# A chunked state-space scan followed by a GELU layer: a rewritten order of steps, and one small product moved to another PSUM bank

## The chip, the cores and the metric

One Trainium2 chip, one of its cores. The metric is the device time of one execution in microseconds (us), lower is better. The engines are TensorE (PE in the profile, with its weight loads apart as PEld), VectorE (DVE), ScalarE (ACT), GpSimd (POOL) and SyncE (SP), which here issues nearly all transfers. Each engine takes its own instructions strictly in the order in which the program was written; the engines wait for one another by semaphores.

## What is computed

A state-space scan over 4 batches, 8 heads and 768 positions, in chunks, with its state carried from chunk to chunk, and then a two-layer network with a GELU on the result. Cut to what matters (the reference's chunk is 32; the kernel uses 128, which gives the same sums):

```python
cum = np.cumsum(log_a[:, :, sl], axis=-1)
L = np.exp(cum[:, :, :, None] - cum[:, :, None, :]) * causal
M = np.einsum('bhin,bhjn->bhij', Cc, Bc) * L
y_intra = np.einsum('bhij,bhjd->bhid', M, xc)
y_inter = np.einsum('bhin,bhnd->bhid', Cc, state) * np.exp(cum)[:, :, :, None]
y[:, :, sl] = y_intra + y_inter
state = decay_full[:, :, None, None] * state + np.sum(Bx, axis=2)
...
h = x @ w_in                # x: y as [3072, 256]; w_in [256, 2048]
g = 0.5 * h * (1.0 + np.tanh(c * (h + 0.044715 * h * h * h)))
out = g @ w_out             # w_out [2048, 256]
```

## The kernel before

Positions are taken in 24 chunks of 128, two chunks to a *unit* u of 256 tokens (12 units, three to a batch). The decays are folded into B and C: C is scaled by the reciprocal of the running product of `a` and B by the product itself, so that the scan of a chunk becomes plain matrix products with a triangular mask.

The kernel schedules itself by hand. Each piece of work is a named *step*. The text `ORDERED` (L19) lists some 600 of them, and the loop at L924 issues them in that order; a suffix `:A`, `:D`, `:P`, `:S` picks ACT, DVE, POOL or SP for a step that can run on several. `~n` issues filler matmuls on TensorE, n units of 128 columns of zeros into the bank `yb` (`fill`, L693); `s1.0.2+4` puts four such units into that step's own bank first. The order within an engine is thus the order of the list, and a step that stands behind a waiting one on its engine waits too. A semaphore wait covers the real dependences, and the bank that a step writes must have been read by those who used it before.

The PSUM banks around the change: two `hp` banks, used in turn by the decay product, the first x and D blocks and all groups of stage 1; one `o_ps` bank (outputs); `ga` and `gb` (G and transposes); one bank `yb` (fillers and Y).

The steps that the text speaks of, with unit u, chunk c = 2u+k and group i:

- `XX.u` (L563) unpacks x of a unit of the first batch by matmul, `XD.u` (L573) adds its state update next to it in the same banks; `xn.c` copies x out to bf16 (L578). A matmul into a bank waits for the reads that were issued before it.
- `G.u` (L595) is C times B, `M.u.0`, `M.u.1` (L605, DVE) apply the triangular mask to its two halves; for unit 0 the second half goes over ACT (`GE`) and POOL (`ME`).
- `S` (L674, L676, DVE) updates the state of a chunk, `SP` (L683, DVE) prepares it for the next chunk.
- `Y.u` (L650 the part from the state, L659 the part within the chunk) writes `yb`; `yev.u` evacuates it to `xm`, the input of stage 1.
- `s1.u.i` (L709) is one of eight groups of four matmuls of the first layer into an `hp` bank, `gelu.u.i` (L713, ACT) empties it; `s2.u.k.q` (L727) is one of four groups of four matmuls of the second layer for a chunk; `oev` copies a finished output, `store` writes it.
- `wi.q.k`, `wo.q.k` cast a part of w_in and w_out to bf16 once it has landed; `castx.u` does so for x.
- `R` (L331) is the long scan of decays, `pe` (L385, L387) the products that start from it, `pp` (L393) spreads them over the partitions on TensorE, `pend` copies them out of PSUM. They are first needed for chunk 4.
- `tp2`, `tp6` (L342), `recip1` (L374), `mul1` (L435), `T1` (L443), `bh1`, `ce1`, `N1`, `bn1` turn decays, scale and transpose B and C of chunks 4 and 5 of the first batch; `mul`, `T`, `E`, `N`, `bn`, `F` do so for batches 2 to 4, where the last two go through DRAM (`store_s`, `turn_s`, `load_s`).

Of these, `s1.u.*` needs `yev.u`, `Y.1` needs `M.1.0`, `M.1.1`, `xn.2`, `xn.3`, `SP.1` and `SP.2`, and `T1.0` needs `mul1.0`, which needs `tp2`.

Of the kernel before, what the change touches and what calls it, by code (L numbers as in the profile page):

```python
# [24 lines left out]
load_bc1.0 xn.2:A ME.3:P ME.2:P pe Y.0 XD.1 pp yev.0.0.2:A S.1.0 load_wo.1 load_bc1.1 SP.1 S.1.1  # L25
load_wo.2 wi.1.1:P M.1.0 wi.2.0:P wo.0.0:D pend:A wo.0.1:P wi.2.1:P SP.2 wi.1.0:A M.1.1 s1.0.0
gelu.0.0 s1.0.1 gelu.0.1 xn.3:A wi.3.1:P s1.0.2+4 gelu.0.2 s1.0.3 s2.0.0.0.o load_wo.3 wo.1.0:P
gelu.0.3 load_bc.1.0 s1.0.4 wi.3.0:A s1.0.5 gelu.0.4 Y.1 tp2 mul1.0 gelu.0.5 yev.1.0.2:A s1.0.6
s1.0.7 gelu.0.6 load_x.2 tp6.0 load_bc.1.1 load_x.3 gelu.0.7 recip1 T1.0 s2.0.1.0.o s1.1.0 bh1:D N1
s1.1.1 wo.1.1:A tp6.3 s2.0.0.1.o wo.2.1:P gelu.1.0 gelu.1.1 mul1.1 tp6.2 T1.1 tp6.1 ce1.1:A ce1.0:A  # L30
wo.2.0:A bn1:D recip.1.4 s2.0.1.1.o s1.1.2 s1.1.3 gelu.1.2 wo.3.0:A wo.3.1:P G.2 gelu.1.3 s2.0.0.2.o
s2.0.1.2.o s2.0.0.3.o castx.2.None:P s2.0.1.3.o load_bc.2.1 M.2.0 mul.1.0 M.2.1 oev.1:A s1.1.4
s1.1.5 T.1.0 load_x.4 oev.0:A s2.1.0.0.o castx.3.None:P s2.1.0.1.o gelu.1.4 SP.3 D.2 gelu.1.5 s1.1.6
S.2.0 SP.4 load_x.5 E.1.0:A N.1 mul.1.1 bn.1:D gelu.1.6 s1.1.7 Y.2 s2.1.0.2.o T.1.1 gelu.1.7
yev.2.0.2:A s1.2.0 s1.2.1 gelu.2.0 E.1.1:D F.1 s2.1.0.3.o s1.2.2 gelu.2.1 gelu.2.2 D.3 load_bc.2.0
oev.2:D G.3 S.3.0 S.3.1 s2.1.1.0.o load_x.6 castx.4.None:P s1.2.3 gelu.2.3 s2.1.1.1.o s2.1.1.2.o
s1.2.4 M.3.1 M.3.0 gelu.2.4 SP.6 s2.1.1.3.o s1.2.5 oev.3:A gelu.2.5 D.4 Y.3 mul.2.1 S.4.0 G.4 s1.2.6
s2.2.0.0.o SP.7 castx.5.None:A yev.3.0.2:A gelu.2.6 S.4.1 s1.2.7 mul.2.0 s2.2.0.1.o s1.3.0
s2.2.0.2.o gelu.2.7 M.4.0 M.4.1 load_x.8 store_s.2.1 gelu.3.0 s1.3.1 s2.2.0.3.o s1.3.2 G.5 gelu.3.1
SP.8 gelu.3.2 store_s.2.0 D.5 Y.4 M.5.1 oev.4:A S.5.0 s1.3.3 s2.2.1.0.o s2.2.1.1.o gelu.3.3 s1.3.4  # L40
s1.3.5 s2.2.1.2.o yev.4.0.2:D s2.2.1.3.o SP.9 SP.10 gelu.3.4 gelu.3.5 s1.3.6 oev.5:A turn_s.2.1
s1.3.7 gelu.3.6 store.1 s2.3.0.0.o M.5.0 gelu.3.7 s2.3.0.1.o store.4 load_s.2 turn_s.2.0 load_x.7
store.0 store.3 store.2 castx.6.None:A s2.3.0.2.o s2.3.0.3.o s1.4.0 gelu.4.0 oev.6:A D.6
castx.7.None:P F.2 Y.5 G.6 S.6.0 S.6.1 s1.4.1 SP.13 s1.4.2 gelu.4.1 s2.3.1.0.o s2.3.1.1.o gelu.4.2
s1.4.3 s1.4.4 M.6.0 M.6.1 gelu.4.3 s2.3.1.2.o s2.3.1.3.o gelu.4.4 oev.7:A s1.4.5 s1.4.6 gelu.4.5
gelu.4.6 yev.5.0.2:D SP.12 s2.4.0.0.o s2.4.0.1.o s1.4.7 D.7 Y.6 G.7 gelu.4.7 load_bc.3.0 load_bc.3.1
mul.3.0 mul.3.1 S.7.0 S.7.1 load_x.9 s1.5.0 gelu.5.0 s2.4.0.2.o s2.4.0.3.o oev.8:A M.7.1
castx.8.None:A M.7.0 s1.5.1 s1.5.2 gelu.5.1 store_s.3.1 yev.6.0.2:D SP.14 s2.4.1.0.o s2.4.1.1.o
s1.5.3 gelu.5.2 s2.4.1.2.o s1.5.4 s2.4.1.3.o gelu.5.3 gelu.5.4 oev.9:A s1.5.5 D.8 Y.7 gelu.5.5
store_s.3.0 load_x.10 load_x.11 store.5 G.8 S.8.0 s1.5.6 s1.5.7 castx.9.None:D gelu.5.6 M.8.1  # L50
gelu.5.7 store.6 s2.5.0.0.o s2.5.0.1.o turn_s.3.0 s1.6.0 s1.6.1 s2.5.0.2.o s2.5.0.3.o gelu.6.0
gelu.6.1 oev.10:D SP.16 s1.6.2 s1.6.3 gelu.6.3 gelu.6.2 s2.5.1.0.o s2.5.1.1.o s2.5.1.2.o s2.5.1.3.o
load_s.3 store.9 turn_s.3.1 s1.6.4 s1.6.5 M.8.0 yev.7.0.2:A oev.11:A SP.15 store.8 gelu.6.4
s2.6.0.0.o F.3 s2.6.0.1.o gelu.6.5 s1.6.6 s1.6.7 gelu.6.6 Y.8 D.9 G.9 S.9.0 SP.18 S.9.1 store.7
gelu.6.7 s2.6.0.2.o s2.6.0.3.o castx.11.None:D oev.12:D s1.7.0 s1.7.1 s2.6.1.0.o gelu.7.0 s2.6.1.1.o
gelu.7.1 s1.7.2 s1.7.3 s2.6.1.2.o s2.6.1.3.o SP.19 oev.13:D M.9.0 gelu.7.2 M.9.1 castx.10.None:P
gelu.7.3 s1.7.4 s1.7.5 s2.7.0.0.o s2.7.0.1.o gelu.7.4 s1.7.6 gelu.7.5 yev.8.0.2:A s2.7.0.2.o s1.7.7
gelu.7.6 Y.9 D.10 S.10.0 S.10.1 G.10 gelu.7.7 M.10.0 s2.7.0.3.o yev.9.0.2:A oev.14:A s1.8.0 s1.8.1
s2.7.1.0.o s2.7.1.1.o gelu.8.0 gelu.8.1 SP.20 s1.8.2 s1.8.3 M.10.1 gelu.8.2 s2.7.1.2.o s2.7.1.3.o
gelu.8.3 s1.8.4 s1.8.5 Y.10 oev.15:A gelu.8.4 D.11 S.11.0 G.11 gelu.8.5 s1.8.6 store.15 s1.8.7  # L60
gelu.8.6 s2.8.0.0.o s2.8.0.1.o gelu.8.7 store.11 store.10 s1.9.0 gelu.9.0 s1.9.1 s2.8.0.2.o
s2.8.0.3.o gelu.9.1 M.11.1 M.11.0 oev.16:D SP.21 SP.22 yev.10.0.2:A s1.9.2 s1.9.3 gelu.9.2
s2.8.1.0.o s2.8.1.1.o gelu.9.3 s1.9.4 store.14 s1.9.5 gelu.9.4 s2.8.1.2.o s2.8.1.3.o gelu.9.5 s1.9.6
# [24 lines left out]
def kernel(  # L88
# [219 lines left out]
    DT, MT, RP = {}, {}, {}  # L308
# [80 lines left out]
            in1=m8.rearrange("p (j o) -> p j o", o=1).to_broadcast([64, 2 * batch, HC]), op=ALU.mult)  # L389

    def f_pp():
        RP[2] = psh.tile([128, 512], FP32, name="hp")
        nc.tensor.matmul(out=RP[2][:, 0:NCH], lhsT=selp[0:64].rearrange("p h n -> p (h n)"),  # L393
                         rhs=pe2.rearrange("p j c -> p (j c)"), start=True, stop=True,
                         skip_group_check=True)
# [567 lines left out]
```

## Time and profile before

| | |
|---|---|
| time, median of 3 runs | 117.17 us (117.15 to 117.68) |
| profiled execution, first to last instruction | 115.1 us; the page gives no other time of it |
| TensorE busy | 109.4 us, 95% |
| ACT, DVE, POOL busy | 75.1, 68.7, 15.1 us |
| chain that ended last, by engine | PE 82%, DMA 8%, SP queue 4% |
| granted TensorE clock, mean | 1.000 |
| TensorE busy in 10.00 to 14.18 us | 3.36 of 4.18 us |
| last output copied out of PSUM from | 112.11 us |

The span runs from the first to the last instruction; the time of a run is longer by what lies around it, 2.1 us if the execution was a median one. A row of the timeline gives start, length, engine, line, operation, written and read tiles, shapes and count; a bracket says how long the engine had been idle before, and who released it. Rows of TensorE overlap, since a matmul's end is that of its last result, while the next is already under way; the pace is read from the starts.

### The profile page before, as it was taken

The numbers are of one execution on the slowest core, as the hardware profiler recorded it, in microseconds if no ns is written. First come the engines' busy times: TensorE is split into PE (matmuls) and PEld (weight loads), VectorE is DVE, ScalarE is ACT, GpSimd is POOL, SyncE is SP. The second block draws the span as 40 slices with busy tenths as digits, with TensorE's granted clock in tenths as the row PEclk, the third lists the DMA queues.
The fourth block names the chain that finished last, engine by engine and source line by source line (L and its number), as shares of the span: only waits on it lengthen the run. The fifth ranks groups of instructions, "written<-read, shape, count | busy, mean of one in ns | idle before, by whom it ended". The sixth has DMA issues, their size and how long they took to land.

```text
span 115.1 us, 3372 instructions
## 1 busy us (share of the span) xinstructions
PE 109.4 (95%) x1425; PEld 92.2 (80%) x1425; DVE 68.7 (60%) x135; ACT 75.1 (65%) x149; POOL 15.1 (13%) x32
## 2 busy tenths in 40 slices
...
GB/s 65 236 280 286 397 293 311 278 84 218 225 109 226 214 64 203 192 147 265 102 158 184 174 178 0 6 0 0 0 50 138 0 49 139 0 0 51 46 103 79
DMA packets 43006, 15.97 MB, mean 139 GB/s; under 512 B 36656, under 2 KB 41456, under 8 KB 42992
## 3 DMA queue, kind: packets, MB, share of 16 engines
q1 hardware_dynamic: 42848, 15.68, 53.9%
q8 instruction: 11, 0.18, 0.6%
q10 hardware_dynamic: 144, 0.08, 0.4%
q14 instruction: 3, 0.02, 0.1%
...
## 4 chain that ended last, share of the span: by engine, by line
PE 82%; DMA 8%; SPq 4%; POOL 1%; issue 1%; ACT 0%
PE hp L709 36%; PE o_ps L727 33%; DMA wf<-in_moe_w_out_dram 8%; PE yb L727 3%; PE ga L595 3%; PE yb L650 2%; PE yb L659 2%; SPq L190 1%; PE hp L628 1%; SPq L162 1%; SPq L159 1%; SPq L150 1%; POOL w_out_sb L316 1%; POOL w_in_sb L316 1%; SPq L183 1%
## 5 line engine op out<-in xcount | busy, mean ns | idle before, releaser
L713 ACT ACTIVATE gT<-hp 128x512 bf16<-128x512 f32 x96 | 53.3, 595 | 24.5 <-PE hp L709 24.0
L709 PE MATMUL hp<-xm,w_in_sb 128*128 128x256 bf16 x384 | 51.9, 273 | 0.5 <-ACT pend L314 0.3
L727 PE MATMUL o_ps<-w_out_sb,gT 128*128 128x256 bf16 x352 | 46.4, 273 | 0.0
L709 PEld LDWEIGHTS <-w_in_sb 128*128 128x128 bf16 x384 | 41.2, 114 | 3.2 <-issue 1.7
L727 PEld LDWEIGHTS <-gT 128*128 128x128 bf16 x384 | 37.0, 98 | 4.7 <-issue 0.8
L318 DVE COPY o_sb<-o_ps 128x256 f32<-128x256 f32 x7 | 3.0, 424 | 22.4 <-PE o_ps L727 18.4
L605 DVE TENSOR_TENSOR m<-ga,tri 128x1024 bf16<-128x1024 f32 x12 | 14.6, 1216 | 0.0
L605 DVE TENSOR_TENSOR m<-gb,tri 128x1024 bf16<-128x1024 f32 x11 | 13.4, 1219 | 0.5 <-PE gb L595 0.5
L697 PE MATMUL yb<-wz 128*128 128x512 bf16 (+2 forms) x24 | 8.2, 491 | 1.1 <-DVE warm L222 1.1
L314 ACT ACTIVATE o_sb<-o_ps 128x256 f32<-128x256 f32 x15 | 5.6, 382 | 4.1 <-PE o_ps L727 3.0
L683 DVE SCALAR_TENSOR_TENSOR sp_new<-s_new,pend,bmask 128x256 bf16<-128x256 f32 x17 | 8.0, 479 | 0.1
L316 POOL CAST x<-x_t 128x512 bf16<-128x512 f32 x5 | 3.2, 648 | 34.9 <-DMA x_t<-in_x_dram 22.9
L676 DVE SCALAR_TENSOR_TENSOR s_new<-s_new,pend,hp 128x64 f32<-128x64 f32 x13 | 3.6, 279 | 5.7 <-PE hp L628 5.5
L697 PEld LDWEIGHTS <-wz 128*128 128x128 bf16 x25 | 2.9, 126 | 5.0 <-issue 3.6
L659 PE MATMUL yb<-m,x 128*32 128x128 bf16 x192 | 6.1, 219 | 0.0
L650 PE MATMUL yb<-ce,sp_new 128*32 128x128 bf16 x160 | 5.3, 220 | 0.0
L595 PE MATMUL ga<-ce,bh 32*128 32x256 bf16 x48 | 4.7, 272 | 0.1
L314 ACT ACTIVATE xm<-yb 128x512 bf16<-128x512 f32 x8 | 4.8, 597 | 0.0
L595 PE MATMUL gb<-ce,bh 32*128 32x256 bf16 x48 | 4.7, 273 | 0.0
L727 PE MATMUL yb<-w_out_sb,gT 128*128 128x256 bf16 x32 | 4.1, 273 | 0.0
L659 PEld LDWEIGHTS <-x 128*32 128x32 bf16 x192 | 3.8, 97 | 0.4 <-issue 0.2
L650 PEld LDWEIGHTS <-sp_new 128*32 128x32 bf16 x160 | 3.0, 96 | 1.0 <-issue 1.0
...
## 6 DMA issues: line engine op xcount, KB each, us to landing
...
wf<-in_moe_w_in_dram SPq DMA_DIRECT2D x4, 512.0 KB, 8.3
wf<-in_moe_w_out_dram SPq DMA_DIRECT2D x4, 512.0 KB, 8.9
...
x_t<-in_x_dram SPq DMA_DIRECT2D x1, 512.0 KB, 4.8
```

The source lines that it names most:

```text
L314: nc.scalar.activation(o, i, AF.Copy)
L316: nc.gpsimd.tensor_copy(out=o, in_=i)
L595: nc.tensor.matmul(out=gbank(g)[:, 256 * k:256 * k + 256], lhsT=bh_of(2 * u + k)[gs], rhs=ce_of(2 * u + k)[gs], start=True, stop=True, til ...
L605: nc.vector.tensor_tensor(out=m_of(u)[:, 2 * i:2 * i + 2].rearrange("p g k e t -> p (g k e) t"), in0=gx[i].rearrange("p g (k t) -> p (g k) ...
L650: nc.tensor.matmul(out=y4[32 * j:32 * j + 32, k, w], lhsT=sp[:, 32 * h:32 * h + 32], rhs=ce_of(gc)[:, h % 2], start=first(j), stop=False, ...
L659: nc.tensor.matmul(out=y4[32 * j:32 * j + 32, k, w], lhsT=X16[u][:, k, 32 * h:32 * h + 32], rhs=m[:, h // 2, h % 2, :], start=first(j), st ...
L676: nc.vector.scalar_tensor_tensor(out=s_new, in0=state[("s", gc - 1)], scalar=pend_of(gc), in1=d, op0=ALU.mult, op1=ALU.add)
L683: nc.vector.scalar_tensor_tensor(out=sp_new.rearrange("p (g d) -> p g d", g=4), in0=(XN[0][:, H * D:H * D + 64] if gc == 0 else state[("s" ...
L697: nc.tensor.matmul(out=t[:, 0:m * 128], lhsT=wz, rhs=w3.to_broadcast([128, m, 128]), start=True, stop=True, skip_group_check=True)
L709: nc.tensor.matmul(out=hp[:, j * T:(j + 1) * T], lhsT=w_in_k[:, w, q, k], rhs=xm[:, w, u * T:(u + 1) * T], start=(w == 0), stop=(w == 1))
L713: nc.scalar.activation(gts[u][:, 2 * i:2 * i + 2], hps.pop((u, i)).rearrange("p (j t) -> p j t", j=2), AF.Gelu_apprx_tanh)
L727: nc.tensor.matmul(out=ops[gc], lhsT=gts[u][:, fi, k * Q:(k + 1) * Q], rhs=w_out_sb[:, fi, :], start=(fi == 0 and (u > 0 or k == 0)), stop ...
```

## The change

Two things. The product `pp` writes the bank `yb` instead of taking an `hp` bank:

```diff
     def f_pp():
-        RP[2] = psh.tile([128, 512], FP32, name="hp")
+        RP[2] = yb
...
-    pp.takes("hp", pd)
+    pp.takes("yb", pd)
```

And the table `ORDERED` is another from the step `xn.0` on, its fifth line, to the end. Some copies and casts also change their engine in it. Its first changed line, before and after:

```diff
-XD.0 load_wo.0 xn.0:A ew.1.2:A SP.0 S.0.0 xn.1:A wi.0.0:A wi.0.1:A R ~13 G.1 S.0.1 load_wi.3 XX.1
+XD.0 load_wo.0 xn.0:A ~6 ~4 ew.1.2:A ~7 SP.0 ~4 ME.3:P S.0.0 xn.1:A ME.2:P S.0.1 wi.0.1:A Y.0
```

What that does to the engines shows in their instructions. First TensorE, between `XD.0` and the first `Y` (`wz` are the zeros of the fillers, `bh` and `ce` the scaled B and C of `G.1`); the difference, - before and + after:

```order
 L697 MATMUL yb<-wz 128x512
 L697 LDWEIGHTS wz
+L697 MATMUL yb<-wz 128x256
+L697 LDWEIGHTS wz
 L697 MATMUL yb<-wz 128x512
 L697 LDWEIGHTS wz
 L697 MATMUL yb<-wz 128x512
 L697 LDWEIGHTS wz
-L697 MATMUL yb<-wz 128x128
-L595 LDWEIGHTS bh_137
-L595 MATMUL ga<-ce_135,bh_137 128x256
```

The fillers there grow from 13 to 21 units, and `G.1`, which stood behind them, is gone from this place. TensorE's steps were `G.1 XX.1 Y.0 XD.1 pp s1.0.0 s1.0.1 s1.0.2+4 s1.0.3 s2.0.0.0 s1.0.4 s1.0.5 Y.1 s1.0.6 s1.0.7 T1.0` and are now `Y.0 XX.1 XD.1 G.1 s1.0.0 pp s1.0.1 s1.0.2+4 s1.0.3 s1.0.4 s1.0.5 Y.1 s1.0.6 s1.0.7 s2.0.0.0 T1.0`.

Next DVE from the first state update to the masks of unit 1 (`s_new` is S, `sp_new` SP, `r_t` R, `pe` the decay products, `x_407` written by xn.2, `m` the mask's result, `rt` a part of tp6):

```order
 L674 COPY s_new<-o_ps 128x64
+L676 SCALAR_TENSOR_TENSOR s_new<-s_new,pendq,hp 128x64
+L683 SCALAR_TENSOR_TENSOR sp_new<-s_new,pendq,bmask 128x256
 L331 SCALAR_TENSOR_TENSOR r_t<-ac,ends 64x384
-L676 SCALAR_TENSOR_TENSOR s_new<-s_new,pendq,hp 128x64
 L385 TENSOR_TENSOR pe_111<-ac,r_t 64x3
 L387 TENSOR_TENSOR pe_112<-pe_111,m_117 64x24
 L676 SCALAR_TENSOR_TENSOR s_new<-s_new,pendq,hp 128x64
+L318 CAST x_407<-hp 128x256
 L683 SCALAR_TENSOR_TENSOR sp_new<-s_new,pendq,bmask 128x256
+L605 TENSOR_TENSOR m<-ga,tri 128x1024
+L605 TENSOR_TENSOR m<-gb,tri 128x1024
```

`S.0.1` and `SP.1` moved ahead of the scan `R`, the copy `xn.2` came over from ACT, and the two masks of unit 1 now follow one another; a cast of w_out that stood between them went to POOL, and one of w_in (`wi.3.1`) came from POOL, behind `S.1.1` and ahead of `tp2`.

Last ACT from the second x copy on (`x_305`, `x_343` and `x_407` are x in bf16 of units 0, 1 and, in the new program, 1; `xm` is written by yev, `gT` by the GELUs):

```order
 L314 ACTIVATE x_305<-hp 128x256
-L314 ACTIVATE w_in_sb<-wf 128x512 x2
-L314 ACTIVATE x_343<-hp 128x256
+L314 ACTIVATE w_in_sb<-wf 128x512
 L314 ACTIVATE xm<-yb 128x2x2x128
-L314 ACTIVATE pend<-hp 128x2x4x3
 L314 ACTIVATE w_in_sb<-wf 128x512
-L713 ACTIVATE gT<-hp 128x512 x2
-L314 ACTIVATE x_343<-o_ps 128x256
-L713 ACTIVATE gT<-hp 128x512 x2
-L314 ACTIVATE w_in_sb<-wf 128x512
+L713 ACTIVATE gT<-hp 128x512
```

One cast of w_in and the copy `xn.2` no longer stand ahead of `yev.0`, and `pend` went behind the fourth GELU. POOL now casts four parts of w_in first (`wi.0.0`, `wi.1.1`, `wi.2.1`, `wi.2.0`), then `wo.0.0`, `wi.3.0` and five of w_out. SP's list is the same in both.

94 lines of the change are left out of this document (47 added, 47 removed).

## Prediction

> **What bounds the kernel now.** I read the table of engine busy time by stretches first, because one number for the whole span hides where TensorE (PE) stands still. The columns are the stretch, its length, then busy microseconds and instruction counts of PE, PEld, DVE, ACT and POOL, and at the end the granted clock, DMA share and GB/s.
>
> ```profile
> 14.18:18.95 4.77, 4.27 (x61) 3.38 (x60) 4.70 (x10) 4.32 (x9) 2.95 (x5) 1.00 1.01 282
> 18.95:112.00 93.05, 93.05 (x1212) 82.89 (x1204) 53.53 (x91) 63.29 (x123) 4.92 (x8) 1.00 0.49 116
> ```
>
> From 18.95 us to the last matmul PE never idles: 93.05 of 93.05 us. A new order can win nothing there, it can only lose. All that can be won lies before 18.95, so the second view is the timeline of PE, and after it the chain of work that ended last for the pace of one stage-1 pair.
>
> ```profile
> 13.25 0.18 PE L573 MATMUL hp<-x4b,bc0s 32*32 32x64 bf16 x1 [0.46 <-ACT x L314]
> ...
> 14.18 1.03 PE L709 MATMUL hp<-xm,w_in_sb 128*128 128x256 bf16 x8 [0.28 <-ACT pend L314]
> ...
> 15.46 0.38 PE L697 MATMUL hp<-wz 128*128 128x512 bf16 x1 [0.25 <-ACT gT L713]
> ...
> 17.51 0.96 PE L709 MATMUL hp<-xm,w_in_sb 128*128 128x256 bf16 x7 [0.25 <-POOL w_in_sb L316]
> ...
> 18.39 0.29 PE L650 MATMUL yb<-ce,sp_new 128*32 128x128 bf16 x8
> ...
> 18.95 1.06 PE L709 MATMUL hp<-xm,w_in_sb 128*128 128x256 bf16 x8
> ...
> 19.85 0.28 PE L443 MATMUL ga<-ident,bc0s 128*128 128x128 bf16 x2
> ```
>
> ```profile
> 22.54 0.87 PE hp L709 x8
> ```
>
> The brackets are the stalls: XD.1 waits 0.46 for xn.2 (13.25), s1.0.0 waits 0.28 (14.18), the filler in s1.0.2 waits for a GELU (15.46), s1.0.4 waits for the cast wi.2.1 on POOL (17.51). The last row says that eight stage-1 matmuls, two groups, take 0.87: a group is 0.44, and a group of stage 2 has the same shape.
>
> My ruler is **the start of T1.0, 19.85**. Before it, both orders have issued exactly the same useful PE work (s1.0.0 to s1.0.7, pp, Y.1, s2.0.0.0), and after it exactly the same is left. So the end moves by as much as T1.0 moves, plus any new stall behind it. The sum is made on this execution, span 115.1; the median of the runs is 117.17, 2.1 more lies around the span, and I move both by the same amount.
>
> **The change, part by part: PE up to s1.0.0.** Spacings of the same blocks in the trace:
>
> ```profile
> 9.08 0.28 PE L595 MATMUL ga<-ce,bh 32*128 32x256 bf16 x2
> ...
> 9.41 0.28 PE L697 MATMUL yb<-wz 128*128 128x256 bf16 x1
> ...
> 9.63 0.28 PE L563 MATMUL o_ps<-x4b,unp 32*128 32x256 bf16 x1
> ...
> 10.16 0.20 PE L573 MATMUL o_ps<-x4b,bc0s 32*32 32x64 bf16 x1
> ...
> 10.40 0.88 PE L697 MATMUL yb<-wz 128*128 128x512 bf16 x4
> ...
> 13.49 0.40 PE L393 MATMUL hp<-pe,selp 64*128 64x24 f32 x2
> ```
>
> and the ACT rows that hand over to PE:
>
> ```profile
> 11.19 0.39 ACT L314 ACTIVATE x<-hp 128x256 bf16<-128x256 f32 x1
> ...
> 11.78 1.15 ACT L314 ACTIVATE w_in_sb<-wf 128x512 bf16<-128x512 f32 x2 [0.19 <-DMA wf<-in_moe_w_in_dram]
> ...
> 14.81 1.09 ACT L713 ACTIVATE gT<-hp 128x512 bf16<-128x512 f32 x2 [0.17 <-PE hp L709]
> ```
>
> Until 10.40 nothing moves, and SP issues all transfers in one order in both kernels, so that I keep the landings of the trace. The fillers there grow from 13 to 21 units of 128 columns; a unit is 0.87/16 = 0.054, so they end at 10.40 + 1.14 = 11.54. Eight units more cost 0.44 of PE, hidden, because Y.0 waits for xn.1 anyway, which ends at 11.58. PE follows ACT by 0.05 (first GELU of the 14.81 pair ends near 15.41, filler at 15.46): Y.0 starts at 11.63. It has three sets of eight where Y.1 has four in 0.56 (18.39 to 18.95): 0.42. Then XX.1 at 12.05, XD.1 0.53 later (9.63 to 10.16) at 12.58, G.1 0.24 later at 12.82, s1.0.0 0.33 later (9.08 to 9.41) at **13.15 instead of 14.18**. XD.1 no longer waits for xn.2, since that copy now stands behind it. Its input is ready: ACT has one cast less ahead of yev.0, so yev.0 runs from about 12.4 to 13.0; wi.0.0 moved to POOL, which is free then. That is 1.03 gained so far.
>
> **The change, part by part: what DVE gives back.** DVE now does S.0.1, SP.1, R, pe, S.1.0, xn.2, SP.2, M.1.0, M.1.1, tp6.0, S.1.1, wi.3.1, tp2, recip1, mul1.0 in this order. Its rows before, and the group row for a copy like xn.2:
>
> ```profile
> L318 DVE COPY o_sb<-o_ps 128x256 f32<-128x256 f32 x7 | 3.0, 424 | 22.4 <-PE o_ps L727 18.4 <-ACT gT L713 4.0
> ```
>
> ```profile
> 11.47 0.21 DVE L674 COPY s_new<-o_ps 128x64 f32<-128x64 f32 x1
> 11.60 0.94 DVE L331 TENSOR_TENSOR_SCAN r_t<-ac,ends 64x384 f32<-64x384 f32 x1
> 12.46 0.25 DVE L676 SCALAR_TENSOR_TENSOR s_new<-s_new,pendq,hp 128x64 f32<-128x64 f32 x1
> 12.63 0.15 DVE L385 TENSOR_TENSOR pe<-ac,r_t 64x3 f32<-64x3 f32 x1
> 12.82 0.18 DVE L387 TENSOR_TENSOR pe<-pe,m 64x24 f32<-64x24 f32 x1
> 13.80 0.28 DVE L676 SCALAR_TENSOR_TENSOR s_new<-s_new,pendq,hp 128x64 f32<-128x64 f32 x1 [0.81 <-PE o_ps L573]
> 14.00 0.48 DVE L683 SCALAR_TENSOR_TENSOR sp_new<-s_new,pendq,bmask 128x256 bf16<-128x256 f32 x1
> ...
> 14.59 1.22 DVE L605 TENSOR_TENSOR m<-ga,tri 128x1024 bf16<-128x1024 f32 x1
> ...
> 15.80 0.43 DVE L318 CAST w_out_sb<-wf 128x512 bf16<-128x512 f32 x1
> ...
> 18.14 0.99 DVE L342 STREAM_TRANSPOSE rt<-r_t 32x64 f32<-32x64 f32 x4
> 19.16 0.52 DVE L435 TENSOR_TENSOR bc0s<-bcf,rt 128x256 bf16<-128x256 f32 x1
> 19.60 0.51 DVE L342 STREAM_TRANSPOSE rt<-r_t 32x192 f32<-32x192 f32 x1
> 20.05 0.20 DVE L374 RECIPROCAL pt<-rt 128x16 f32<-128x16 f32 x1
> ```
>
> Two rules from them: an instruction that needs nothing of its predecessor starts about 0.08 before that one ends (11.68 against 11.60), one that does starts 0.04 after (12.78, 12.82). From S.0.0, which ends at 11.68 in both orders: S.0.1 11.72, SP.1 12.01, R 12.41, pe 13.39 to 13.76, S.1.0 13.68, **xn.2 13.88 to 14.30**, SP.2 14.22, M.1.0 14.62, M.1.1 15.76 to 16.98, tp6.0 16.90, S.1.1 17.33, wi.3.1 17.53 to 17.96, tp2 17.88, recip1 18.91, **mul1.0 19.03 to 19.55**.
>
> Now PE against this. pp needs pe: 13.86 (PE follows DVE by 0.10: 14.08 to 14.18 before). Its two passes, 0.40 with their drain, are hidden: s1.0.1 takes the hp bank that xn.2 frees, so it starts only at 14.40. From there PE and ACT play ping-pong over two hp banks: a GELU starts 0.63 after its group (14.18 to 14.81) and lasts 0.60, and the next group on that bank 0.05 later. So s1.0.2 15.06 (behind its filler, 0.22, as before), s1.0.3 15.68, s1.0.4 16.34, s1.0.5 16.96, with some 0.2 of idle ahead of each of the last three. Before, s2.0.0.0 stood in such a gap; it now comes later and its 0.44 are not hidden. The POOL stall of 17.51 goes, since both wi.2 casts now precede wo.0. Y.1 at 17.40 needs M.1.1 (16.98), in time; s1.0.6 needs wi.3.1: 18.06; s1.0.7 18.50; s2.0.0.0 18.93; PE would be at T1.0 at 19.37. But T1.0 transposes what mul1.0 writes: 19.55 + 0.10 = **19.65**. So of the 1.03 only 0.20 are left: DVE, which had slack, now sets the pace, because R, pe and xn.2 stand ahead of both M.1 on it.
>
> **POOL next to DVE.** One row makes me take off half of that:
>
> ```profile
> 14.51 0.61 POOL L316 CAST w_in_sb<-wf 128x512 bf16<-128x512 f32 x1 [0.74 <-DMA wf<-in_moe_w_in_dram]
> ...
> 15.83 0.87 POOL L316 CAST w_out_sb<-wf 128x512 bf16<-128x512 f32 x1 [0.71 <-DMA wf<-in_moe_w_out_dram]
> ...
> 16.14 0.83 DVE L683 SCALAR_TENSOR_TENSOR sp_new<-s_new,pendq,bmask 128x256 bf16<-128x256 f32 x1
> ```
>
> and the issue of wi.3 with, from the view of transfers, its time from issue to landing:
>
> ```profile
> 6.74 0.76 SPq L190 DMA_DIRECT2D wf<-in_moe_w_in_dram  x1
> ```
>
> ```profile
> wf<-in_moe_w_in_dram SPq DMA_DIRECT2D x1, 512.0 KB, 10.3
> ```
>
> SP.2 took 0.83 against 0.48 for SP.1, beside a POOL cast that overlapped it by 0.56 (16.14 to 16.70): 0.35 lost. In the new order wi.3.1 on DVE meets wi.3.0 on POOL: wi.3 lands at 6.74 + 10.3 = 17.04, the POOL cast runs to about 17.71, the DVE cast wants 17.53: overlap 0.18. Bounds: nothing, or the whole 0.35. By the nearest row, in proportion, 0.18 x 0.35/0.56 = 0.1; I take 0.1, T1.0 at 19.75, **0.10 gained**. The Trainium skill, "SBUF — State Buffer", section "Who interferes with whom", says that DVE and GpSimd share one pair of SBUF ports under an exclusive lock, so that the later of two such instructions blocks until the first is done. The rows here agree that something is lost, but 0.35 of 0.56 is not the whole overlap; by that rule the loss here would be 0.18 instead of 0.1, T1.0 19.83 and the gain 0.02.
>
> **Behind T1.0** I looked for places where the new order puts a step directly behind what it needs. One shows: D.2 now follows s1.1.6, s1.1.7 and six transposes, on the bank that the GELU of s1.1.6 frees. PE gets there 0.44 + 0.44 + 0.33 = 1.21 after s1.1.6 began (six transposes at 0.054 as a 128-column unit), the bank is free after 0.63 + 0.60 + 0.05 = 1.28: a stall of 0.07. Elsewhere copies of outputs and casts of x move from ACT and POOL to DVE, which is idle for 39.5 of the 93.05 us; that hides them, and where it does not it costs. Sum: -0.10 + 0.07 = **-0.03**, span 115.1, time 117.1.
>
> **The rivals.**
> 1. *PE sets T1.0, not DVE* (19.37; DVE's rows shrink a little or overlap more): -0.48 + 0.07, 116.8. For it: all DVE terms are single rows. Against it: fifteen instructions would have to run 0.3 shorter together.
> 2. *The whole head start is kept* (1.03): 116.1. It needs mul1.0 done near 18.7, 0.8 ahead of the sum of its rows. Only if the GELU ping-pong and DVE are both much faster than shown.
> 3. *Slower: DVE is held by POOL's casts.* The same mechanism at full price: the casts of w_in and w_out now stand closer together on POOL, and SP.2, wi.3.1 and mul1.0 each meet one. At 0.35 for the first two plus 0.1 for the third, T1.0 comes at 19.65 + 0.8 = 20.45, 0.60 late, and with D.2 the time is 117.8. It decides for the slower side once DVE loses more than 0.2 in all between 14.2 and 19.6. For it: the 0.83 row. Against it: SP.2 starts at 14.22, before POOL's cast of wi.2 (14.51), so POOL would be the one to wait.
> 4. *A stall behind 19.85 in the rewritten table*, where before there was none: a copy on DVE that waits for PE or for a DMA holds the M or F queued behind it. No row of before prices it; one lost stage-1 group is 0.44, two are 0.87, 117.5 to 118.0.
>
> That the change does not do what it says is excluded by its order, in which Y.0 precedes XX.1 and Y.1 follows s1.0.5.
>
> **How the numbers follow.** Forecast (DVE sets T1.0, within 0.2 of 19.75) 0.51; rival 1 0.18; rival 2 0.09; rival 3 0.12; rival 4 0.10. A measurement of this kernel can tell about 0.5%, 0.59 us, from no change. Faster by more: rival 2 and a third of rival 1, which lies close to that bound, 0.15. Slower by more: most of rival 3 and of rival 4, 0.19. Within: 0.66. The range reaches from a little under rival 1 to rival 3: 116.6 to 117.8, and leaves out rival 2 and the longer stalls of rival 4.
>
> **What would show it.** In the profile of the changed kernel: Y.0 near 11.6 and s1.0.0 near 13.2; s1.0.1 waiting for a DVE copy until about 14.4; DVE busy without a gap from 11.5 to 19.6; T1.0 waiting for DVE at L435, between 19.6 and 19.9; nearly no idle PE after it. I am wrong if T1.0 waits for nothing, if DVE rows between 14 and 19.6 are longer than quoted, or if PE shows waits of 0.3 or more behind 20.

## The result and the profile after

| | before | after |
|---|---|---|
| time, median of 11 runs | 117.44 us | 118.20 us |
| ratio to before, 95% interval | | **1.0066** (1.0039 to 1.0093) |
| the same kernel once more, against 28 runs of before | | 1.0078 (1.0051 to 1.0105) |
| profiled execution shown here: time, span | | 118.39 us, 116.7 us |

The change made the kernel **slower by 0.7%, 0.8 us**. Forecast was 117.1 us with a range of 116.6 to 117.8: the time lies above the range, on the side to which 0.19 had been given. Part of the distance is the base: over 11 runs the kernel before has 117.44, 0.27 more than the 117.17 from which the forecast was made; with that added the top of the range would be 118.07, still below 118.20. The first execution that was profiled ran at a lower TensorE clock (120.31 us, mean 0.986), so the rows below are from the second set, `again`, at full clock.

The waits of TensorE in `again` (line waited for, total, times, longest):

```profile
PE yb L697 <- DVE warm L222: 1.1, 1, 1.1
PE yb L393 <- DVE pe L387: 0.6, 1, 0.6
PE ga L443 <- DVE bc0s L435: 0.6, 1, 0.6
PE hp L425 <- DVE cz L409: 0.4, 1, 0.4
PE ga L595 <- ACT ce L452: 0.2, 1, 0.2
```

Three are new, and all three come from DVE's queue (`ce1.0` on ACT follows `ce1.1` on DVE). The waits that the old order had ahead of `XD.1`, `s1.0.0` and `s1.0.4` are gone. The same on TensorE's timeline, from the first `G.0` to `G.2`:

```profile
8.92 0.28 PE L595 MATMUL ga<-ce,bh 32*128 32x256 bf16 x2
...
11.49 0.30 PE L659 MATMUL yb<-m,x 128*32 128x128 bf16 x8
...
13.05 0.63 PE L709 MATMUL hp<-xm,w_in_sb 128*128 128x256 bf16 x4
14.29 0.40 PE L393 MATMUL yb<-pe,selp 64*128 64x24 f32 x2 [0.62 <-DVE pe L387]
14.82 0.63 PE L709 MATMUL hp<-xm,w_in_sb 128*128 128x256 bf16 x4
...
20.77 0.28 PE L443 MATMUL ga<-ident,bc0s 128*128 128x128 bf16 x2 [0.61 <-DVE bc0s L435]
...
24.00 0.28 PE L595 MATMUL ga<-ce,bh 32*128 32x256 bf16 x2 [0.24 <-ACT ce L452]
```

In this execution `G.0` starts 0.16 earlier than in the profile of before (8.92 against 9.08), before anything that the change touches; for a comparison with the forecast 0.16 is added. `Y.0` then is at 11.65 (forecast 11.63) and `s1.0.0` at 13.21 (13.15): the head start is there. At `s1.0.1` it is lost already, 14.98 instead of 14.40, and `T1.0` comes at 20.93 instead of 19.75. Why, DVE's rows tell, those that answer to the rows of the prediction, and the two that carry on from there:

```profile
11.94 0.67 DVE L683 SCALAR_TENSOR_TENSOR sp_new<-s_new,pendq,bmask 128x256 bf16<-128x256 f32 x1
12.54 0.94 DVE L331 TENSOR_TENSOR_SCAN r_t<-ac,ends 64x384 f32<-64x384 f32 x1
13.52 0.15 DVE L385 TENSOR_TENSOR pe<-ac,r_t 64x3 f32<-64x3 f32 x1
13.71 0.53 DVE L387 TENSOR_TENSOR pe<-pe,m 64x24 f32<-64x24 f32 x1
...
15.08 1.21 DVE L605 TENSOR_TENSOR m<-ga,tri 128x1024 bf16<-128x1024 f32 x1
...
17.95 0.77 DVE L318 CAST w_in_sb<-wf 128x512 bf16<-128x512 f32 x1
...
19.94 0.77 DVE L435 TENSOR_TENSOR bc0s<-bcf,rt 128x256 bf16<-128x256 f32 x1
...
21.30 0.69 DVE L435 TENSOR_TENSOR bc0s<-bcf,pt 128x256 bf16<-128x256 f32 x1
...
27.39 0.95 DVE L475 TENSOR_TENSOR bc<-bc_t,rt 128x768 bf16<-128x768 f32 x1
```

and POOL's casts in the same stretch:

```profile
11.73 0.61 POOL L316 CAST w_in_sb<-wf 128x512 bf16<-128x512 f32 x1 [0.45 <-DMA wf<-in_moe_w_in_dram]
13.59 0.61 POOL L316 CAST w_in_sb<-wf 128x512 bf16<-128x512 f32 x1 [1.25 <-DMA wf<-in_moe_w_in_dram]
14.93 1.26 POOL L316 CAST w_in_sb<-wf 128x512 bf16<-128x512 f32 x2 [0.72 <-DMA wf<-in_moe_w_in_dram]
...
17.57 0.87 POOL L316 CAST w_in_sb<-wf 128x512 bf16<-128x512 f32 x1 [0.76 <-DMA wf<-in_moe_w_in_dram]
18.39 2.05 POOL L316 CAST w_out_sb<-wf 128x512 bf16<-128x512 f32 x3
```

Put the two lists side by side. `SP.1` begins at 11.94 within the cast that ends at 12.34, the second `pe` at 13.71 within the one that ends at 14.20, `wi.3.1` at 17.95 within the one that ends at 18.44, `mul1.0` at 19.94 within the three that end at 20.44. Each is longer than its shortest row in any profile here (0.46, 0.17, 0.41, 0.36), by 0.21, 0.36, 0.36 and 0.41: 1.34 us up to `T1.0`, where 0.1 had been allowed. This profile is the worst case of the table further down: up to `mul1.0` the other four there with all casts lost 0.36 to 1.01. `mul1.1` adds 0.32 (shortest row 0.37). DVE has no gap in all this time, so none of it is absorbed.

### The profile page after: what moved, and what is told of

It is laid out like the page before. It is cut to its first block, busy times and chain, and to the rows that moved or that the text cites. A ratio compares the mean times of both kernels' runs of the same rounds, so it can differ in the third digit from the quotient of the medians.

```text
span 118.6 us, 3372 instructions
## 1 busy us (share of the span) xinstructions
PE 111.6 (94%) x1427; PEld 92.6 (78%) x1427; DVE 75.3 (64%) x146; ACT 71.1 (60%) x137; POOL 15.2 (13%) x33
## 4 chain that ended last, share of the span: by engine, by line
PE 85%; DVE 5%; ACT 1%; issue 0%; DVEq 0%
PE hp L709 37%; PE o_ps L727 33%; PE ga L595 3%; PE yb L727 3%; PE yb L650 2%; PE yb L659 2%; DVE cz L409 1%; DVE r_t L331 1%; PE hp L628 1%; DVE sp_new L683 1%; PE yb L697 1%; ACT gT L713 1%; DVE pe L387 0%; PE o_ps L563 0%; DVE pe L385 0%; DVE s_new L676 0%
## 5 line engine op out<-in xcount | busy, mean ns | idle before, releaser
L709 PE MATMUL hp<-xm,w_in_sb 128*128 128x256 bf16 x384 | 53.1, 278 | 0.3 <-ACT gT L713 0.2
L727 PE MATMUL o_ps<-w_out_sb,gT 128*128 128x256 bf16 x352 | 47.3, 273 | 0.0
L709 PEld LDWEIGHTS <-w_in_sb 128*128 128x128 bf16 x384 | 41.7, 115 | 3.8 <-issue 1.9
L318 DVE COPY o_sb<-o_ps 128x256 f32<-128x256 f32 x14 | 5.9, 423 | 19.3 <-PE o_ps L727 19.2
L697 PE MATMUL yb<-wz 128*128 128x512 bf16 (+3 forms) x26 | 8.5, 481 | 1.1 <-DVE warm L222 1.1
L314 ACT ACTIVATE o_sb<-o_ps 128x256 f32<-128x256 f32 x8 | 3.1, 385 | 3.9 <-PE o_ps L727 3.5
L316 POOL CAST x<-x_t 128x512 bf16<-128x512 f32 x3 | 1.8, 613 | 23.8 <-DMA x_t<-in_x_dram 13.0
L318 DVE CAST xm<-yb 128x512 bf16<-128x512 f32 x4 | 2.7, 684 | 2.8 <-PE yb L659 2.8
```

What stands on the lines that cost most here:

```text
L314: nc.scalar.activation(o, i, AF.Copy)
L318: nc.vector.tensor_copy(out=o, in_=i)
L697: nc.tensor.matmul(out=t[:, 0:m * 128], lhsT=wz, rhs=w3.to_broadcast([128, m, 128]), start=True, stop=True, skip_group_check=True)
L709: nc.tensor.matmul(out=hp[:, j * T:(j + 1) * T], lhsT=w_in_k[:, w, q, k], rhs=xm[:, w, u * T:(u + 1) * T], start=(w == 0), stop=(w == 1))
L727: nc.tensor.matmul(out=ops[gc], lhsT=gts[u][:, fi, k * Q:(k + 1) * Q], rhs=w_out_sb[:, fi, :], start=(fi == 0 and (u > 0 or k == 0)), stop ...
```

## The experiments

Every kernel is timed against the kernel before, and every ratio is to it. Unless another base is named, each is the changed kernel with one edit. Line numbers of the experiments differ by a few from those above, since the edits move lines.

**`again`: is it only the clock?** No edit.

> The changed kernel once more, unchanged, for a profile at full clock. Theory A (POOL's casts of w_in hold the scan R and the two pe instructions on DVE): R takes about 1.4 instead of 0.94, the two pe about 0.5 each instead of 0.15 and 0.18, the first product of pp waits about 1.2 for pe, and the loss of about 0.7 stands although the clock stays at 1.0. Theory C (only the clock that falls in PE's gap costs time): at full clock T1.0 comes within 0.3 of the forecast and the time is level with before.

Measured 1.0078 (1.0051 to 1.0105) at full clock: theory C falls, the loss needs no fall of the clock. Theory A's sizes fit only in part: `R`, which had taken 1.37 in the first profile, kept its 0.94 here, one `pe` of two was hit, and `SP.1`, `wi.3.1`, `mul1.0` and `mul1.1` were hit instead. Which instruction meets a cast changes from one execution to the next, since the casts start when their transfers land.

**`casts_act`: three casts off POOL.**

```diff
...
-yev.0.0.2:A SP.1 R pe XX.1 XD.1 S.1.0 wi.1.0:A G.1 xn.2:D SP.2 wi.0.0:P s1.0.0 gelu.0.0 wi.1.1:P pp
+yev.0.0.2:A SP.1 R pe XX.1 XD.1 S.1.0 wi.1.0:A wi.1.1:A G.1 xn.2:D SP.2 wi.0.0:P s1.0.0 gelu.0.0 pp
...
-load_wi.3 M.1.0 M.1.1 xn.3:A tp6.0 S.1.1 s1.0.1 s1.0.2+4 gelu.0.1 wi.2.1:P wi.3.1:D wi.2.0:P s1.0.3
+load_wi.3 M.1.0 M.1.1 xn.3:A wi.2.1:A wi.2.0:A tp6.0 S.1.1 s1.0.1 s1.0.2+4 gelu.0.1 wi.3.1:D s1.0.3
```

> The casts wi.1.1, wi.2.0 and wi.2.1 go from POOL to ACT; DVE and PE keep their order. Theory A: R is back at 0.94 and pe at 0.15 and 0.18, pp starts about 1.1 earlier, and the ratio to before falls from 1.0066 to about 0.998 (0.995 to 1.002; ACT has 1.9 more to do, most of it in gaps). Rival B (R is long because of its new place or its neighbours on DVE, or pp's wait comes from PE's queue): R and pe stay at 1.4 and 0.5, the ratio stays at 1.005 or more.

Measured 1.0045 (1.0007 to 1.0082), above theory A's range of 0.995 to 1.002. `R` and `pe`, and TensorE's new wait in the same kernel:

```profile
13.25 0.94 DVE L331 TENSOR_TENSOR_SCAN r_t<-ac,ends 64x384 f32<-64x384 f32 x1
14.23 0.15 DVE L385 TENSOR_TENSOR pe<-ac,r_t 64x3 f32<-64x3 f32 x1
14.41 0.18 DVE L387 TENSOR_TENSOR pe<-pe,m 64x24 f32<-64x24 f32 x1
```

```profile
17.40 1.09 PE L709 MATMUL hp<-xm,w_in_sb 128*128 128x256 bf16 x8 [0.94 <-ACT gT L713]
```

These rows are short, as theory A says, but a part of the gain went into a wait for ACT, whose GELUs now stand behind two casts. In this profile DVE also waited 1.04 ahead of `wi.3.1` for the transfer of its input, and `SP.1` met a cast that was left (0.74 instead of 0.46). Inconclusive as to size.

**`R_late`: the scan behind the masks.**

```diff
...
-SP.1 R pe XX.1 XD.1 S.1.0
+SP.1 XX.1 XD.1 S.1.0
...
-s1.0.0 gelu.0.0 wi.1.1:P pp load_wi.3 M.1.0 M.1.1 xn.3:A tp6.0
+s1.0.0 gelu.0.0 wi.1.1:P load_wi.3 M.1.0 M.1.1 R pe xn.3:A tp6.0
...
-wi.2.0:P s1.0.3
+wi.2.0:P s1.0.3 pp
```

> R and pe move on DVE from behind SP.1 to behind M.1.1, and pp on PE behind s1.0.3; the casts stay on POOL. Theory A: xn.2, SP.2 and both M.1 come about 2.3 earlier, s1.0.1 starts within 0.8 of s1.0.0, PE has no wait of 1.2; R may still be stretched by a cast but nothing on PE waits for it before T1.0. Ratio to before 0.994 to 1.001. If the later part of the new table costs the time and not this place (theory D), the ratio stays at 1.005 or more although the 1.2 wait is gone.

Measured 1.0154 (1.0085 to 1.0224), a miss. `s1.0.1` followed `s1.0.0` at once, as expected, but `pp`, which I had put ahead of `s1.0.4`, now waited for a `pe` that came later still:

```profile
17.98 0.40 PE L392 MATMUL yb<-pe,selp 64*128 64x24 f32 x2 [2.07 <-DVE pe L386]
```

The edit moved the wait instead of removing it, and made it longer.

**`pp_late`: only the product moves on TensorE.**

```diff
...
-s1.0.0 gelu.0.0 wi.1.1:P pp load_wi.3
+s1.0.0 gelu.0.0 wi.1.1:P load_wi.3
...
-wi.2.0:P s1.0.3
+wi.2.0:P s1.0.3 pp
```

> Only pp moves on PE, from ahead of s1.0.1 to behind s1.0.3. Theory A: s1.0.1 needs the bank that xn.2 frees, and xn.2 stands behind pe on DVE, so s1.0.1 starts as late as in the changed kernel; ratio to before 1.004 to 1.009. Rival B (pp's place ahead of s1.0.1 on PE is what costs): s1.0.1 starts about 1 us earlier, ratio 0.996 to 1.001.

Measured 1.0068 (1.0034 to 1.0103): no change against the changed kernel. `s1.0.1` waits all the same, for `xn.2`, which stands behind `pe` on DVE:

```profile
14.87 0.63 PE L708 MATMUL hp<-xm,w_in_sb 128*128 128x256 bf16 x4 [0.83 <-DVE x L317]
```

So the place of `pp` costs nothing of its own, and rival B falls. No run puts `pp` back into an `hp` bank, so the new bank is not tested by itself. In `again` it causes no wait: `pp` waits for `pe`, and `Y.1`, the next to write `yb`, starts at 17.94 without one.

**`small_after`, `small_before`, and again as `small_after2`, `small_before2`: POOL's casts made small.** The casts on POOL keep their places and waits, but nine of them (six in the kernel before) copy 8 columns instead of 512; zeros stand in for the other weights. The first pair wrote these zeros partly on POOL and DVE:

> The changed kernel, in which the nine casts that POOL has ahead of T1.1 (wi.0.0, wi.1.1, wi.2.0, wi.2.1, wi.3.0, wo.0.0, wo.0.1, wo.1.0, wo.1.1) copy 8 columns instead of 512 of each block; the rest of these weights is zero, written early by idle engines. Order and waits stay. Theory A (POOL's casts stretch DVE's instructions, and DVE sets T1.0): SP.1 is back at 0.49, pe at 0.18, wi.3.1 at 0.43, mul1.0 at 0.52; T1.0 starts 1.0 to 1.2 earlier than in the profile at full clock, near 19.75; the ratio to before falls from 1.007 to 0.997 to 1.001. Rival (the new DVE order itself, or the table behind T1.0, costs the time): T1.0 stays past 20.3 and the ratio at 1.004 or more.

> The kernel before, in which the six casts that POOL has ahead of T1.0 (wi.1.1, wi.2.0, wi.2.1, wi.3.1, wo.0.1, wo.1.0) copy 8 columns instead of 512, with zeros for the rest as in small_after. Theory A: DVE had slack here, so only PE's wait of 0.28 for wi.2.1 goes: ratio to before 0.996 to 1.000. If the kernel before gained as much as the changed one (0.7% or more), the casts would not be what tells the two apart.

Measured 1.0127 (1.0076 to 1.0178) and 0.9992 (0.9960 to 1.0025). The first is spoilt by the edit itself: the first scaling on DVE met the zeros written on POOL (0.99 instead of 0.23), `G.0` began at 10.09, a microsecond late, and that went into the time. The second pair writes the zeros on ACT alone (`SI` lists the casts that are cut, `fl` their places in the weights, `z4` is the zeros of the fillers; the casts of w_out are cut in the same way):

```diff
 def f_wi(q, k, eng):
-    copy(eng, w_in_sb[:, k, q * 512:(q + 1) * 512], WF[("i", q)][:, k])
+    n = 8 if (q, k) in SI else 512
+    copy(eng, w_in_sb[:, k, q * 512:q * 512 + n], WF[("i", q)][:, k, 0:n])
...
 def f_pendq(eng):
+    for o in fl[:7]:
+        nc.scalar.activation(o, z4, AF.Copy)
     copy(eng, pendq, RP[0][:, 0:R4])
```

> small_after again, with the zeros written by ACT alone, in time in which it is idle, so that the start is not disturbed: the nine casts of POOL copy 8 columns of 512. Theory A+E: no instruction of DVE is stretched up to mul1.0, T1.0 near 19.7, G.2 still waits for ce1.0 and starts near 22.8 on the clock of the kernel before, 0.4 later than there; ratio to before 1.002 to 1.005, against 1.007 for the changed kernel. If POOL's casts were all of the loss: 0.997 to 1.001. If none of it: 1.006 or more.

> The kernel before with its six casts of POOL cut to 8 columns of 512 in the same way. DVE has slack there: only PE's wait of 0.28 for wi.2.1 can go; ratio to before 0.996 to 1.000.

Measured **0.9980 (0.9943 to 1.0018) and 0.9980 (0.9934 to 1.0025): with small casts the two orders are level**, where they are 0.7% apart with full ones. The two intervals together leave some 0.6% of doubt on that. The time of `small_after2` lies where the expectation had "POOL's casts were all of the loss" (0.997 to 1.001), not where theory A+E had it (1.002 to 1.005). DVE's rows in `small_after2`, and the start of `G.0` and `G.2` on TensorE:

```profile
12.34 0.49 DVE L694 SCALAR_TENSOR_TENSOR sp_new<-s_new,pendq,bmask 128x256 bf16<-128x256 f32 x1
...
13.91 0.18 DVE L398 TENSOR_TENSOR pe<-pe,m 64x24 f32<-64x24 f32 x1
...
17.80 0.41 DVE L320 CAST w_in_sb<-wf 128x512 bf16<-128x512 f32 x1
...
19.42 0.36 DVE L446 TENSOR_TENSOR bc0s<-bcf,rt 128x256 bf16<-128x256 f32 x1
...
26.58 0.95 DVE L486 TENSOR_TENSOR bc<-bc_t,rt 128x768 bf16<-128x768 f32 x1
```

```profile
9.32 0.28 PE L606 MATMUL ga<-ce,bh 32*128 32x256 bf16 x2
...
19.84 0.28 PE L454 MATMUL ga<-ident,bc0s 128*128 128x128 bf16 x2
...
23.20 0.28 PE L606 MATMUL ga<-ce,bh 32*128 32x256 bf16 x2 [0.64 <-ACT ce L463]
```

The first four rows are back at their short form. `T1.0` is at 19.84, with `G.0` 0.24 later than in the profile of before: 19.60 on its clock, where the forecast without any loss to POOL had 19.65. But `G.2` waits 0.64 all the same. The larger part of that is a cast too, the next one on POOL behind the nine (`wo.2.1`), which still copies 512 columns and meets `SP.3`:

```profile
20.69 0.61 POOL L318 CAST w_out_sb<-wf 128x512 bf16<-128x512 f32 x1 [1.50 <-DMA wf<-in_moe_w_out_dram]
20.71 0.87 DVE L694 SCALAR_TENSOR_TENSOR sp_new<-s_new,pend,bmask 128x256 bf16<-128x256 f32 x1
```

That row is 0.41 longer than the shortest of its form (0.46). The two groups ahead of `G.2` start at 21.52 and take 0.87 by the pace of the starts, so `G.2` could have come at 22.39 and came 0.81 later; without the stretch 0.40 is left. In `again`, `xn_act` and `dve_more` the same difference is 0.41. So the casts are the loss up to `T1.0`; between `T1.0` and `G.2` some 0.4 is a second matter, which the new order has without any cast.

**`tp6_late`, `tp6_all`: transposes out of the way.** From the start of `G.2` to the end, 92.70 us pass in `again` (116.7 - 24.00) and in `small_after2` (115.9 - 23.20). `G.2` waits for `ce1.0`, which follows `ce1.1`, and ahead of `ce1.1` on DVE stand `tp6.0`, `tp6.3` and `tp6.1`, 0.5 each. `tp6_late` moves the first two behind `mul1.1`, `tp6_all` all three behind `bn1`:

```diff
...
-M.1.0 M.1.1 xn.3:A tp6.0 S.1.1
+M.1.0 M.1.1 xn.3:A S.1.1
...
-Y.1 tp6.3 gelu.0.5 mul1.1 wi.3.0:P
+Y.1 gelu.0.5 mul1.1 tp6.0 tp6.3 wi.3.0:P
```

> The changed kernel with the transposes tp6.0 and tp6.3 on DVE moved behind mul1.1; nothing else. Theory A (DVE's queue sets T1.0 and T1.1): mul1.0 ends 0.45 earlier and mul1.1 0.97 earlier; PE's wait ahead of T1.0 falls from 0.6 to 0.2 or less, T1.1 does not wait; ratio to before 1.000 to 1.003. Rival (PE's own wait for pe at pp sets T1.0): T1.0 does not move, ratio 1.005 or more.

> The changed kernel with tp6.0, tp6.3 and tp6.1 on DVE moved behind bn1, so that ce1.1 no longer stands behind them. Theory E (from G.2 on PE never waits, 92.70 from G.2's start to the end in every profile so far, and G.2 waits for ce1.0, which waits for ce1.1 at the end of DVE's queue): G.2 does not wait any more, it starts near 22.5 on the clock of the kernel before, and the ratio to before falls to 0.998 to 1.002, although tp6_late, which moved two of these transposes only as far as ahead of ce1.1, is at 1.0103. Rival (T1.0's start decides, as forecast): as tp6_late, ratio 1.005 or more.

Measured 1.0103 (1.0052 to 1.0153) and 1.0107 (1.0048 to 1.0167): no gain in either, so theory A's range for the first (1.000 to 1.003) and theory E's for the second (0.998 to 1.002) are both missed. `T1.0` no longer waits in the first, and instead `G.2` waits longer; in the second `G.2` does not wait, and instead `T.1.0` (the first transposes of the second batch) does. The rows are TensorE's of `tp6_late`, then DVE's and TensorE's of `tp6_all`:

```profile
23.68 0.28 PE L595 MATMUL ga<-ce,bh 32*128 32x256 bf16 x2 [1.08 <-ACT ce L452]
```

```profile
21.73 0.48 DVE L454 TENSOR_SCALAR ce<-gb,par 128x256 bf16<-128x256 bf16 x1 [0.64 <-PE gb L443]
```

```profile
28.66 0.51 PE L484 MATMUL ga<-ident,bc 128*128 128x128 bf16 x6 [0.74 <-DVE bc L475]
```

The wait only changes its place, and where DVE's queue was reordered so far that `ce1.1` had to wait for TensorE (the middle row), the gap of 0.64 came on top. The profile of `tp6_late` has stretched rows as well (1.08, in the table below). That made theory F: from `SP.0` to `mul.1.0` (the row of L475) DVE's queue is the bound, and it is its length that counts, not the place of an instruction in it.

**`xn_act`, `dve_more`: one instruction less, one more.** `xn_act` has `xn.2:A` ahead of `S.1.0`; `dve_more` copies the same source once more on DVE:

```diff
 def f_xn(c, eng):
     copy(eng, X16[u][:, k], XN[c][:, 0:H * D])
+    if c == 2:
+        copy(eng, spare, XN[c][:, 0:H * D])
```

> The changed kernel with xn.2 on ACT (ahead of S.1.0) instead of DVE; nothing else. Theory F (DVE's queue from SP.0 to mul.1.0 has no gap, so its length sets the time): 0.3 to 0.4 less, ratio to before 1.002 to 1.005. If only the place of single instructions counts: as the changed kernel, 1.006 or more, since pp still waits for pe.

> The changed kernel with one more copy of 0.41 on DVE, right behind xn.2 (the same source, into a spare tile that nobody reads). Theory F: the time grows by 0.35 to 0.45, ratio to before 1.009 to 1.012. If DVE's queue has slack: 1.0066 to 1.0075.

Measured 1.0066 (1.0030 to 1.0102) and 1.0093 (1.0058 to 1.0128). By the times alone nothing is decided: the first lies in the range of its rival, the second in theory F's, and each interval holds numbers of both ranges. The profiles tell more, once the three things that vary are taken apart: when `G.0` starts, how much the casts stretch, and the rest of the queue. Starts of `G.0` and the rows of `mul.1.0`, of `xn_act` and of `dve_more`:

```profile
9.02 0.28 PE L595 MATMUL ga<-ce,bh 32*128 32x256 bf16 x2
```

```profile
26.93 0.95 DVE L475 TENSOR_TENSOR bc<-bc_t,rt 128x768 bf16<-128x768 f32 x1
```

```profile
10.12 0.28 PE L598 MATMUL ga<-ce,bh 32*128 32x256 bf16 x2
```

```profile
27.72 0.95 DVE L476 TENSOR_TENSOR bc<-bc_t,rt 128x768 bf16<-128x768 f32 x1
```

| kernel | `G.0` | `mul.1.0` ends | from `G.0` to there | stretched | left | from there to the end |
|---|---|---|---|---|---|---|
| `again` | 8.92 | 28.34 | 19.42 | 1.66 | 17.76 | 88.36 |
| `pp_late` | 9.29 | 27.55 | 18.26 | 0.37 | 17.89 | 88.35 |
| `tp6_late` | 9.10 | 28.02 | 18.92 | 1.08 | 17.84 | 88.38 |
| `small_after2` | 9.32 | 27.53 | 18.21 | 0.41 | 17.80 | 88.37 |
| `xn_act` | 9.02 | 27.88 | 18.86 | 1.32 | 17.54 | 88.32 |
| `dve_more` | 10.12 | 28.67 | 18.55 | 0.46 | 18.09 | 88.33 |

"Stretched" is the sum over the queue of what a row has beyond the shortest row of the same instruction in any profile, where that is more than 0.07. The span is known to 0.1 only, so that the last column is good to 0.05; it is constant within 0.06. And "left" is 17.76 to 17.89 for the four kernels with the same instructions on DVE, 0.3 less with one copy taken off, 0.3 more with one added (a copy of 0.41 that starts 0.08 before its predecessor ends is worth 0.33). For these six profiles, one of each kernel, theory F holds: **span = start of `G.0` + 17.8 + what the casts stretch + 88.36**.

**`best1`, `best2`, `best3`, `best4`: orders from the theories.** All four have `xn.2` on ACT. `best1` is `tp6_late` with `pp` behind `s1.0.3`:

> As tp6_late, and xn.2 goes back to ACT (behind the copy of the first y), and pp stands behind s1.0.3. PE then needs neither pe nor a DVE copy for s1.0.1, and DVE has 0.41 less. Theory A: s1.0.1 starts within 0.8 of s1.0.0, DVE reaches mul1.0 about 0.9 earlier than in the changed kernel, T1.0 near 19.8; ratio to before 0.995 to 1.000, the fastest of the orders so far. If the ratio stays above 1.003, something other than DVE's queue holds the changed order.

Measured 1.0074 (1.0040 to 1.0108): the row of `xn.2` on ACT waited 1.43 for `S.1.0`, which stood ahead of it in the table and behind `R` and `pe` on DVE.

> A version from the theory: as tp6_all, and R moves behind M.1.1, pe behind mul1.0, pp behind N1, pend behind the GELU after it, SP.3 behind tp6.1, xn.2 back to ACT ahead of S.1.0, wi.3.1 behind tp2. DVE then reaches mul1.0 about 1 us earlier, and neither s1.0.1 nor anything ahead of T1.0 waits for pe. Theory E: G.2 at 21.5 to 22.2 on the clock of the kernel before, whose own work has it at 22.4; ratio to before 0.990 to 0.999. If R and wi.3.1 meet POOL's casts at full price again, 1.000 to 1.003.

Measured 1.0180 (1.0130 to 1.0230), the slowest of all. With `R` behind the masks DVE stood idle while it waited for `xn.2` to be done (0.95) and for TensorE ahead of `ce1.1` (0.81), and `s1.0.6` waited for `wi.3.1`, which I had put behind `tp2`:

```profile
19.15 0.95 PE L707 MATMUL hp<-xm,w_in_sb 128*128 128x256 bf16 x7 [0.91 <-DVE w_in_sb L316]
```

Its premise, that early transposes and an early scan are what hold DVE up, was that of `tp6_all` and fell with it. `best3` keeps `R` in its place, where it fills a gap; its edit in the table, with `best4`'s two further swaps below it:

```diff
...
-SP.1 R pe XX.1 XD.1 S.1.0 wi.1.0:A G.1 xn.2:D SP.2
+SP.1 R XX.1 XD.1 xn.2:A S.1.0 wi.1.0:A G.1 SP.2
...
-load_bc1.0 tp2 recip1 load_wo.1 gelu.0.3 mul1.0
+load_bc1.0 recip1 load_bc1.1 gelu.0.3 mul1.0 tp6.0
...
-N1 bn1:D gelu.1.1
+N1 bn1:D pp gelu.1.1 pend:A tp6.1 SP.3
...
-wi.0.1:A Y.0 yev.0.0.2:A SP.1 R XX.1 XD.1 xn.2:A S.1.0
+Y.0 yev.0.0.2:A wi.0.1:A SP.1 R XX.1 XD.1 S.1.0 xn.2:A
```

> The changed kernel with DVE's queue shortened and its gaps filled: xn.2 on ACT, R stays behind SP.1 (it fills the wait for S.1.0), pe goes behind mul1.1 and pp behind N1, tp6.0 behind mul1.0, tp6.3 behind pe, tp6.1 and SP.3 behind bn1, wi.3.1 behind tp2, the load of the second C ahead of that of wo.1. Theory F: mul.1.0 ends 0.7 to 1.0 earlier than in the changed kernel, PE waits less than 0.3 ahead of G.2 and T.1.0; ratio to before 0.996 to 1.002. Above 1.004 theory F misses something.

> As best3, with S.1.0 issued ahead of xn.2, and on ACT the first copy of y ahead of the cast wi.0.1, so that DVE does not wait for ACT ahead of S.1.0. Theory F: the gap of 0.47 in DVE's queue goes and mul.1.0 ends 0.3 to 0.7 earlier than in best3, counted from G.0; ratio to before 0.996 to 1.001 (best3 had 1.0029). If PE's own work is the bound by then, the ratio stays near 1.000.

Measured 1.0029 (1.0000 to 1.0058) and 1.0027 (0.9979 to 1.0074). By the medians `best3` takes back more than half of the loss, but its interval still overlaps that of the changed kernel (1.0039 to 1.0093). `S.1.0` in `best3` and in `best4` (here `ce1.1` too):

```profile
13.54 0.28 DVE L673 SCALAR_TENSOR_TENSOR s_new<-s_new,pendq,hp 128x64 f32<-128x64 f32 x1 [0.47 <-ACT x L311]
```

```profile
13.92 0.25 DVE L672 SCALAR_TENSOR_TENSOR s_new<-s_new,pendq,hp 128x64 f32<-128x64 f32 x1
...
21.41 0.48 DVE L450 TENSOR_SCALAR ce<-gb,par 128x256 bf16<-128x256 bf16 x1 [0.61 <-PE gb L439]
```

In `best4` the gap of 0.47 is closed, as meant, but DVE now waits 0.61 for TensorE at `ce1.1`, and the time stays. In this profile TensorE waits for nothing behind the filler of `s1.0.2`, which starts at 15.64: there it is the bound again. The time is level with the kernel before within its interval. No order that was tried beats the kernel before.

## Why the prediction was wrong, step by step

- **The head start, 1.03 at `s1.0.0`: right.** 13.21 against 13.15, and 13.15 is where the fillers, `Y.0`, `XX.1`, `XD.1` and `G.1` had been laid out. The extra fillers are hidden, as said.
- **DVE busy without a gap, and `T1.0` set by DVE: right.** `small_after2` gives it with POOL's casts made small: 19.60 against 19.65. That it is so close is in part luck, since the forecast's 0.52 for `mul1.0` was itself a stretched row; with the plain 0.36 it would have been 19.49.
- **POOL next to DVE, +0.1: the step that failed.** The mechanism was named, the size was not: 1.34 up to `mul1.0` in `again`, 1.66 up to `mul.1.0`. The price was nearly right: 0.35 for an overlap of 0.56 is 0.63 of it, and the four meetings in `again` lost 1.34 of 1.88, which is 0.71. What was wrong is the count: one meeting of 0.18, with POOL's casts and DVE's instructions at fixed times, against four of 0.40 to 0.50. In the new order POOL is busy 7.11 of the 11.42 us ahead of `T1.0`, and DVE has no gap, so that meetings are the rule and only their places are chance:

```profile
9.35:20.77 11.42, 9.95 (x190) 6.50 (x190) 10.74 (x24) 9.27 (x20) 7.11 (x11) 1.00 1.02 331
```

- **"After it exactly the same is left", with only D.2 (0.07) late behind `T1.0`: wrong as well.** From `T1.0` to the end it is 115.1 - 19.85 = 95.25 before and 116.7 - 20.77 = 95.93 after, 0.68 more. D.2 shows no wait. By the starts, 0.41 of it lies ahead of `G.2`, and 0.29 ahead of `T1.1`, which comes at 22.05 instead of 21.76 behind the stretched `mul1.1` (21.30 to 21.99). In `small_after2` it is 115.9 - 19.84 = 96.06, 0.81 more than before, of which 0.41 is the stretch of `SP.3`; the other 0.40 is the loss ahead of `G.2`, where 0.07 had been allowed in all. `G.2` waits because the new table has one stage-2 group between `T1.0` and it instead of three, and DVE's queue goes on without a gap to `ce1.1`. I had looked only at the banks behind TensorE's steps, and had counted DVE's idle 39.5 us over the whole rest of the kernel, where none of it lies in the 8 us that matter.
- **The rivals.** Rival 3, "DVE is held by POOL's casts", is what happened, with 0.12 and a price of 0.8 by `T1.0` (117.8 us); it measured 1.34 there in the profile shown. Two of its three places (`wi.3.1`, `mul1.0`) were hit; `SP.2` was not, `SP.1` and `pe` were. Rival 4's stall behind the table's first part exists, and 0.40 is near its smallest price (0.44), but there TensorE waits for DVE's queue, not DVE for TensorE or a transfer. Rivals 1 and 2 needed DVE to be faster than its rows.

Does the account close? The kernel before takes 115.1 - 9.08 = 106.02 us from `G.0` to the end. The new order without any stretch would take 17.8 + 88.36 = 106.16, 0.14 more: level, as forecast and as the pair with small casts measured. The two parts give the same: `T1.0` 0.25 earlier (19.60 against 19.85) and 0.40 lost ahead of `G.2`. The five profiles with full casts and the changed kernel's queue, give or take one copy (`again`, `pp_late`, `tp6_late`, `xn_act`, `dve_more`), have 0.98 of stretch on average, so 1.1 us of loss would be expected; 0.8 to 0.9 was measured. The kernel before has stretched rows too (0.37 on `SP.2`, 0.16 on `mul1.0`), but TensorE never waits for them, and behind 18.95 it waits for nothing at all, so that they cost nothing. What stays open: how a single execution's casts fall, which no run here controlled, and the difference of 0.2 to 0.3 between the loss expected from five profiles and the one measured.
